# The expert layers as 2 x 2 block products: seven products in place of eight, taken from a growing PSUM bank

## The chip, the cores and the metric

One core of a Trainium2 chip runs the whole program. The metric is the device time of one execution in microseconds (us), lower is better. An execution has five engines that each work through a queue of their own in order: TensorE (PE), VectorE (DVE), ScalarE (ACT), GpSimd (POOL) and the queue that issues transfers (SP). Results of TensorE go to PSUM, which has eight banks here.

## The reference, cut to what matters

An attention block (a linear recurrence with decay, 4 batches, 8 heads, 768 steps, head size 48) gives 3072 rows `x` of 384. Each row is routed to one of eight experts, and the expert is two dense layers in float32:

```
idx  = argmax(cos(x, expert_emb) / tau);  gate = softmax(...)[idx]
for e in range(8):                       # D = 384, F = 1024
    rows = idx == e
    h = maximum(x[rows] @ w1[e], 0)      # (rows x 384) @ (384 x 1024)
    out[rows] = gate[rows] * (h @ w2[e]) # (rows x 1024) @ (1024 x 384)
```

## The kernel before

The attention phase comes first and is not touched, except that two experts ("early", `EARLY = 2`) begin there with rows that are already known. After it `experts` (L1107) goes through eight experts. Each has room for `CAPS[e]` rows: 384, 384, 432, 416, 400, 384, 384, 384. Rows are gathered from DRAM into tiles `G` of 128 rows (`gather`, L994, POOL).

For one expert the work is:

- `turn_x` (L1027): nine or twelve TensorE transposes turn the gathered rows into `xT` (feature on the partitions), for three blocks `m` of 128 features through two PSUM banks `Y`, each copied out by DVE (L1039).
- `layer1` (L1052): for each of eight blocks `f` of 128 hidden units, three matmuls (one per `m`) with 128 x 128 weights of `w1` and all rows of the expert as moving columns, then a Relu on ACT out of PSUM into `hT` (L1049).
- `layer2` (L1074): with 384 rows, for each tile of 128 rows eight matmuls over `f`, each 384 columns wide (L1081), then `finish`: DVE multiplies by the gate (L1062) and POOL scatters the 128 rows to `out` by an indirect transfer (L1063). With more than 384 rows the product is taken turned round (weights `w2` stationary, rows moving, L1089), copied to `yT` by DVE (L1092), and `turn_out` (L1095) transposes four tiles back (L1101) and calls `finish` for each, after the next expert's first layer.

A float32 matmul is two TensorE instructions in the trace, and so are its weight loads (PEld). A transpose is one. The early experts' rows beyond 256 and the transposes for expert 2 come just before `layer2` of experts 0 and 1. From there the order of work on every engine is the program's order, written by hand: layer2(0), layer2(1), then for e = 2 to 7 layer1(e), turn_out(e-1), turn_x(e+1), gathers for e+2, layer2(e), and the loads of the weights of e+2 (`weights`, L975, on SP). The attention phase orders its work by a `Plan`: a list of (planned time, function) that is sorted and emitted. Its planned times only fix the order on each queue.

Of the kernel before, what the change touches and what calls it, by code (L numbers as in the profile page):

```python
# [9 lines left out]
F32 = mybir.dt.float32  # L10
I32 = mybir.dt.int32
ACT = mybir.ActivationFunctionType
ALU = mybir.AluOpType
# [3 lines left out]
B, H, S, D = 4, 8, 768, 48  # L17
DM, E, F = H * D, 8, 1024
N = B * S
# [5 lines left out]
NK = DM // 128  # L25
# [254 lines left out]
def rings(k):  # L280

    nc, pool = k.nc, k.aconst

    def ring(name, count, shape, pad=None, pool=pool):
        out = []
        for i in range(count):
            t = pool.tile(shape, F32, name=f"{name}{i}")
            if pad is not None:
                nc.gpsimd.memset(t[:, :, :, D:DP], 0.0)
            out.append(t)  # L290
        return out
# [12 lines left out]
    k.T = [[pool.tile([128, 2, NP, D], F32, name=f"T{bp}_{i}") for i in range(2)] for bp in range(2)]  # L304

    flat = lambda x: x.rearrange(f"q {' '.join('abcde'[: len(x.shape) - 1])} -> q ({' '.join('abcde'[: len(x.shape) - 1])})")
    k.spare = []
    for x in map(flat, (*k.R, *k.K, *k.Rw, *k.Kw[::-1])):
        k.spare += [x[:, i : i + 384] for i in range(0, x.shape[1] - 383, 384)]
    k.early_x = [  # L310
        flat(of(k.RT, t))[:, 0 : NK * 384].rearrange("q (m i) -> q m i", m=NK) for t in (TURNS - 3, TURNS - 2)
    ]
    k.T1 = [pool.tile([128, 2, NP, D], F32, name=f"Tmid{bp}") for bp in range(2)]
    k.peek = pool.tile([128, 2], F32, name="peek")
    k.sq = ring("sq", 1, [128, DM])
    k.ssq = [k.const.tile([128, B], F32, name=f"ssq{i}") for i in range(2)]
# [648 lines left out]
    plan.emit()  # L965


def weight_tiles(k):
    return (
        k.wp.tile([128, NK, F], F32, name="w1", tag="w1"),  # L970
        k.wp.tile([128, NF, DM], F32, name="w2", tag="w2"),
    )


def weights(k, j, which, pieces=None, paced=False):  # L975
# [28 lines left out]


def x_of(k, e, m):
    return (k.early_x[e] if e < EARLY else k.xT[e % 2])[:, m, :]


def h_of(k, e, f):  # L1010
    return k.spare[e * NF + f] if e < EARLY else k.hT[e % 2][:, f, :]


def turn_tile(k, e, t):

# [11 lines left out]
def turn_x(k, e):  # L1027
    if e < EARLY:
        for t in range(AHEAD, TILES[e]):
            turn_tile(k, e, t)  # L1030
        return
    for m in range(NK):
        ps = k.Y[m % 2]
        for t in range(TILES[e]):
            G, r = k.G[(e % 2) * TM + t], rows_in(e, t)
            k.nc.tensor.transpose(  # L1036
                ps[:, t * 128 : t * 128 + r], G[0:r, m * 128 : (m + 1) * 128], k.ident[0:r, 0:r]
            )
        k.nc.vector.tensor_copy(x_of(k, e, m)[:, 0 : CAPS[e]], ps[:, 0 : CAPS[e]])  # L1039


def first_layer(k, e, f, cols):
    w1 = k.weights[e][0]
    ps = (k.D[3], k.Y[1], k.D[0], k.D[1])[f % 4][:, 0 : cols.stop - cols.start]
    for m in range(NK):
        k.last = k.nc.tensor.matmul(  # L1046
            ps, w1[:, m, f * 128 : (f + 1) * 128], x_of(k, e, m)[:, cols], start=(m == 0), stop=(m == NK - 1)
        )
    k.nc.scalar.activation(h_of(k, e, f)[:, cols], ps, ACT.Relu)  # L1049


def layer1(k, e):  # L1052
    cols = slice(AHEAD * 128 if e < EARLY else 0, CAPS[e])
    for f in range(NF):
        first_layer(k, e, f, cols)


def finish(k, e, t, ps):

    n = rows_in(e, t)  # L1060
    y = k.gp.tile([128, DM], F32, name="y", tag="y")
    k.nc.vector.tensor_scalar_mul(y[0:n], ps[0:n], k.lists[0:n, e, 1, t : t + 1])  # L1062
    k.nc.gpsimd.indirect_dma_start(  # L1063
        out=k.out[:, :], out_offset=IndirectOffsetOnAxis(ap=k.goes[0:n, e, t : t + 1], axis=0),
        in_=y[0:n, :], in_offset=None, bounds_check=N - 1, oob_is_err=False,
    )


def next_bank(k):
    k.turn = 1 - k.turn  # L1070
    return k.U[k.turn]


def layer2(k, e):  # L1074

    n, w2 = CAPS[e], k.weights[e][1]
    if n % 128 == 0:
        for t in range(TILES[e]):
            ps = next_bank(k)[:, 0:DM]
            for f in range(NF):  # L1080
                k.nc.tensor.matmul(  # L1081
                    ps, h_of(k, e, f)[:, t * 128 : (t + 1) * 128], w2[:, f, :], start=(f == 0), stop=(f == NF - 1)
                )
            finish(k, e, t, ps)
        return
    for m in range(NK):
        ps = next_bank(k)[:, 0:n]
        for f in range(NF):
            k.nc.tensor.matmul(  # L1089
                ps, w2[:, f, m * 128 : (m + 1) * 128], h_of(k, e, f)[:, 0:n], start=(f == 0), stop=(f == NF - 1)  # L1090
            )
        k.nc.vector.tensor_copy(k.yT[:, m, 0:n], ps)  # L1092


def turn_out(k, e):  # L1095
    if CAPS[e] % 128 == 0:
        return
    for t in range(TILES[e]):
        ps, n = next_bank(k)[:, 0:DM], rows_in(e, t)
        for m in range(NK):  # L1100
            k.nc.tensor.transpose(  # L1101
                ps[0:n, m * 128 : (m + 1) * 128], k.yT[:, m, t * 128 : t * 128 + n], k.ident
            )
        finish(k, e, t, ps)


def experts(k):  # L1107
    nc = k.nc
    k.turn = 1
    k.xT = [k.gp1.tile([128, NK, max(CAPS)], F32, name=f"xTe{i}") for i in range(2)]  # L1110
    k.hT = [k.gp1.tile([128, NF, max(CAPS)], F32, name=f"hT{i}") for i in range(2)]
    k.yT = k.gp1.tile([128, NK, max(CAPS)], F32, name="yT")
    for e in range(EARLY):
        turn_x(k, e)
    for e in range(EARLY):
        for t in range(TILES[EARLY + e]):
            gather(k, EARLY + e, t)
    nc.gpsimd.drain()
    for e in range(EARLY):
        layer1(k, e)  # L1120
    turn_x(k, EARLY)
    for e in range(E):
        if e >= EARLY:
            layer1(k, e)
            turn_out(k, e - 1)
            if e + 1 < E:
                turn_x(k, e + 1)
            if e + 2 < E:
                for t in range(TILES[e + 2]):
                    gather(k, e + 2, t)  # L1130
            nc.gpsimd.drain()
        if e == E - 1:
            k.tc.mark_branch_hint_location("rest", "LikelyTaken")
        layer2(k, e)
        if e + 2 < E:
            k.weights.append(weight_tiles(k))
            for i in range(2):
                weights(k, e + 2, i)
        if e == EARLY:
            k.left = nc.values_load(k.flag[0:1, 0:1], min_val=0, max_val=1)  # L1140


def needs(k, first):
# [244 lines left out]
def kernel(  # L1388
# [20 lines left out]
    def pool(name, bufs, **kw):  # L1409
        return ctx.enter_context(tc.tile_pool(name=name, bufs=bufs, **kw))  # L1410
# [6 lines left out]
    n.turned = ((n.D[0], n.D[1]), (n.D[2], n.D[3]))  # L1417
    n.rows = n.U
    n.const = pool("const", 1)
    n.wp = pool("wp", 2)  # L1420
# [5 lines left out]
    n.weights = [weight_tiles(n) for _ in range(2)]  # L1426
    n.expert = {}
    n.G = [n.const.tile([128, DM], F32, name=f"G{i}") for i in range(2 * TM)]

# [41 lines left out]
```

## Time and profile before

Three runs took 426.38, 427.07 and 429.15 us, median 427.07. The profiled execution took 427.70 us; its span, from the first instruction to the last, is 425.9 us, so 1.8 us lie around it.

| | busy us | share of span |
|---|---|---|
| PE (matmuls) | 399.3 | 94% |
| DVE | 147.4 | 35% |
| POOL | 124.7 | 29% |
| ACT | 103.1 | 24% |

Busy time of PE in stretches of the span, with DVE and ACT beside it:

| stretch (us) | work | PE busy | DVE | ACT |
|---|---|---|---|---|
| 178 to 211 | transposes for expert 2, layer2(0), layer2(1) | 32.97 of 33.0 | 4.91 | 0.28 |
| 230.4 to 247.9 | layer2(2), 432 rows | 17.50 of 17.5 | 1.81 | 0.00 |
| 264.66 to 268.76 | turn_out(2), turn_x(4) | 3.62 of 4.1 | 3.33 | 0.52 |
| 356.5 to 372 | layer1(6) | 15.50 of 15.5 | 0.62 | 3.43 |
| 404.4 to 420 | layer2(7) | 15.60 of 15.6 | 1.24 | 0.49 |
| 420 to 425.9 | last gate product, last scatter | 0.09 of 5.9 | 0.62 | 0.00 |

A duration of a matmul in the rows is longer than the distance to the next one, because matmuls overlap: 384 columns show 486 ns, and begin every 322 ns. Where TensorE is full, distances are what counts. The granted TensorE clock is 1.00 in all these stretches.

### The profile page before, as it was taken

To read this page: it belongs to the slowest core of one execution; us is meant where nothing else is said; L and a number is where in the kernel's file an instruction comes from. 1 tells how busy PE (TensorE), PEld (TensorE's weight loads), DVE (VectorE), ACT (ScalarE), POOL (GpSimd) and SP (SyncE) were. 2 spreads that over 40 slices of the span, in tenths; PEclk is the share of its full clock that TensorE was granted. 3 is DMA by queue.
4 is the path that set the end of the run, shared out by engine and by line. 5 is a ranking of instruction groups with operands and counts; after the bars stand their busy time and mean duration, and the time that the engine had idled before them with its cause. 6 is when DMAs were issued, how large, how long until landed. Compare 5 with 4: busy or idle time off the path is not lost. (4 is left out here: it accounts for less than half of the span.)

```text
span 425.9 us, 10753 instructions
## 1 busy us (share of the span) xinstructions
PE 399.3 (94%) x4512; PEld 276.7 (65%) x4512; DVE 147.4 (35%) x428; ACT 103.1 (24%) x263; POOL 124.7 (29%) x167
## 2 busy tenths in 40 slices
PE   7879889799998899999999999999999999999994
PEld 3767778798987788855555555555555565555552
DVE  7957577588887540111101100310310211011000
ACT  1345545545555223300021012002101100200200
POOL 2756556275622232211240000240032013201001
PEclk9999999899999899999999999999999999999999
DMA  9999777576125577605564040424416235200001
GB/s 168 189 185 219 163 166 153 118 155 146 42 77 170 145 240 245 209 18 170 203 215 148 0 148 8 179 83 143 164 44 202 69 136 159 99 20 35 0 22 41
DMA packets 94683, 54.28 MB, mean 127 GB/s; under 512 B 77955, under 2 KB 89266, under 8 KB 94626
## 3 DMA queue, kind: packets, MB, share of 16 engines
q1 hardware_dynamic: 88658, 43.67, 37.6%
q0 software_dynamic: 3264, 9.44, 6.6%
q8 instruction: 37, 0.61, 0.6%
q10 hardware_dynamic: 2704, 0.40, 0.6%
q14 instruction: 20, 0.16, 0.1%
HBM read 44.20 MB, written 9.58 MB: 126 GB/s over the span
## 5 line engine op out<-in xcount | busy, mean ns | idle before, releaser
L1063 POOL DMA_INDIRECT out_dram<-y,goes x27 | 26.5, 981 | 204.4 <-DVE y L1062 153.3
L1046 PE MATMUL ps<-xTe,w 128*128 128x384 f32 (+3 forms) x216 | 75.5, 499 | 0.0
L1049 ACT ACTIVATE hT<-ps 128x384 f32<-128x384 f32 (+3 forms) x36 | 18.1, 504 | 184.6 <-PE ps L1046 184.6
L1062 DVE TENSOR_SCALAR y<-pu,lists_sorted 128x384 f32<-128x384 f32 (+3 forms) x27 | 16.1, 614 | 131.9 <-PE pu L1081 83.9
L1046 PEld LDWEIGHTS ps<-xTe,w 128*128 128x128 f32 x216 | 41.0, 190 | 31.5 <-issue 11.9
L1089 PE MATMUL pu<-hT,w 128*128 128x432 f32 (+2 forms) x144 | 51.0, 514 | 0.0
L1081 PE MATMUL pu<-w,hT 128*128 128x384 f32 x144 | 46.9, 486 | 0.0
L1089 PEld LDWEIGHTS pu<-hT,w 128*128 128x128 f32 x144 | 27.1, 190 | 22.0 <-issue 15.3
L1081 PEld LDWEIGHTS pu<-w,hT 128*128 128x128 f32 x144 | 27.2, 190 | 18.5
L999 POOL DMA_INDIRECT G<-xs,take x23 | 23.2, 1008 | 26.2 <-PE py L1019 10.1
L348 POOL TENSOR_TENSOR Rw<-R,rpow 128x384 f32<-128x384 f32 x22 | 22.8, 1036 | 22.7 <-PE ps L390 20.9
L1046 PE MATMUL ps<-RT,w 128*128 128x256 f32 (+1 forms) x144 | 27.1, 340 | 0.4 <-DVE RT L1022 0.4
L1046 PE MATMUL py<-xTe,w 128*128 128x384 f32 (+3 forms) x72 | 26.1, 499 | 0.0
L1039 DVE COPY xTe<-py 128x384 f32<-128x384 f32 (+3 forms) x18 | 10.0, 568 | 44.9 <-PE py L1036 44.4
L390 PE MATMUL ps<-RT,KT 48*64 48x128 f32 x768 | 24.3, 273 | 0.5 <-DVE RT L377 0.5
L1046 PEld LDWEIGHTS ps<-RT,w 128*128 128x128 f32 x144 | 22.6, 197 | 2.5 <-ACT Rw L1049 0.6
L343 POOL TENSOR_TENSOR Kw<-K,kpow 128x384 f32<-128x384 f32 x22 | 23.5, 1066 | 0.0
L390 PEld LDWEIGHTS ps<-RT,KT 48*64 48x64 f32 x768 | 20.9, 133 | 3.1 <-issue 2.1
L1092 DVE COPY yT<-pu 128x432 f32<-128x432 f32 (+2 forms) x9 | 5.3, 591 | 45.4 <-PE pu L1089 45.4
L1046 PEld LDWEIGHTS py<-xTe,w 128*128 128x128 f32 x72 | 13.7, 190 | 10.5 <-issue 4.0
L364 PE MATMUL ps<-ident,Rw 128*128 128x128 f32 x96 | 15.6, 286 | 4.8 <-POOL T L453 2.2
L377 DVE TENSOR_TENSOR RT<-ps,uw 128x512 f32<-128x512 f32 x24 | 16.5, 688 | 9.8 <-ACT RT L371 9.7
(239 smaller groups left out, 532.5 us busy)
## 6 DMA issues: line engine op xcount, KB each, us to landing
w<-in_moe_w_dram SPq DMA_DIRECT2D x24, 512.0 KB, 4.7
w<-in_moe_w_dram SPq DMA_DIRECT2D x32, 384.0 KB, 4.9
K<-in_k_dram SPq DMA_DIRECT2D x24, 192.0 KB, 3.5
V<-in_v_dram SPq DMA_DIRECT2D x24, 192.0 KB, 3.7
xs<-X SPq DMA_DIRECT2D x24, 192.0 KB, 2.5
R<-in_r_dram SPq DMA_DIRECT2D x22, 192.0 KB, 4.4
out_dram<-y,goes POOLq DMA_INDIRECT x27, 2.6
R<-in_r_dram ACTq DMA_DIRECT2D x2, 192.0 KB, 5.2
```

The lines of the kernel that those rows point to most:

```text
L343: q.tensor_mul(of(k.Kw, t)[:, u, :, 0:D], of(k.K, t)[:, u], k.kpow)
L348: ins = q.tensor_mul(of(k.Rw, t)[:, u, :, 0:D], of(k.R, t)[:, u], k.rpow)
L364: k.nc.tensor.transpose(bank[:, p * C : (p + 1) * C], pair(src[:, u], p), k.ident)
L377: k.nc.vector.tensor_mul(of(k.RT, t)[:, u, :, :, 1, :], k.turned[u][0].rearrange("q (p s i) -> q p s i", p=NP, s=2), k.uw[:, :, None, None ...
L390: ins = k.nc.tensor.matmul(k.D[2 * u + par][halves(s), p * C : (p + 1) * C], KT[rows, u, p, halves(s)], RT[rows, u, p, s].rearrange("q j i ...
L999: k.nc.gpsimd.indirect_dma_start(out=G[0:n, :], out_offset=None, in_=k.xs[0:rows, :], in_offset=IndirectOffsetOnAxis(ap=(k.take_first if f ...
L1046: k.last = k.nc.tensor.matmul(ps, w1[:, m, f * 128 : (f + 1) * 128], x_of(k, e, m)[:, cols], start=(m == 0), stop=(m == NK - 1))
L1049: k.nc.scalar.activation(h_of(k, e, f)[:, cols], ps, ACT.Relu)
L1062: k.nc.vector.tensor_scalar_mul(y[0:n], ps[0:n], k.lists[0:n, e, 1, t : t + 1])
L1063: k.nc.gpsimd.indirect_dma_start(out=k.out[:, :], out_offset=IndirectOffsetOnAxis(ap=k.goes[0:n, e, t : t + 1], axis=0), in_=y[0:n, :], in ...
L1081: k.nc.tensor.matmul(ps, h_of(k, e, f)[:, t * 128 : (t + 1) * 128], w2[:, f, :], start=(f == 0), stop=(f == NF - 1))
L1089: k.nc.tensor.matmul(ps, w2[:, f, m * 128 : (m + 1) * 128], h_of(k, e, f)[:, 0:n], start=(f == 0), stop=(f == NF - 1))
```

## The change

Each layer is cut into 2 x 2 blocks and multiplied with seven block products in place of eight (Strassen's scheme in Winograd's form). Sums and differences of blocks of both operands are made by DVE: `S1`, `T1` for layer 1, `S2`, `T2` for layer 2. In layer 1 only two of the three feature blocks `m` can be paired; the third adds four plain products to a group of four `f` (`group`), so that a group has eleven products of two matmuls at half the rows (192 to 216 columns). In layer 2 two tiles of 128 rows are paired, and halves of 192 output columns: seven products of four matmuls. The third tile, or the 144 to 176 rows beyond 256, stays plain (`third`, `columns`).

The partial sums that several outputs share are not multiplied again. A PSUM bank "a" grows through the products, and ACT copies it at three states to `kept` (`keep`); two more banks "b" and "c" take the rest, and DVE adds `kept` to them on the way out (`add`), three additions in a group. Relu of those three outputs then runs on ACT from SBUF in place. The banks come from a ring of six (`ring_bank`).

The copies of the transposed rows go from DVE to ACT (`copy_x`), and `turn_m` places the third block of transposes after the first matmuls of layer 2. `turn_out` handles two tiles in place of four. All of this stands in one `Plan` with planned times. Weight buffers are fixed pairs, `h` of odd experts and `S2` lie in attention's `RT` buffers.

```diff
-    k.spare = []
-    for x in map(flat, (*k.R, *k.K, *k.Rw, *k.Kw[::-1])):
-        k.spare += [x[:, i : i + 384] for i in range(0, x.shape[1] - 383, 384)]
+    k.spare_two = [
+        flat(x)[:, 0:768].rearrange("q (f i) -> q f i", f=2) for x in (*k.R, *k.K, *k.Rw, *k.Kw[::-1])
+    ]
...
-def weight_tiles(k):
-    return (
-        k.wp.tile([128, NK, F], F32, name="w1", tag="w1"),
-        k.wp.tile([128, NF, DM], F32, name="w2", tag="w2"),
-    )
+def weight_tiles(k, i):
+    return k.wp.tile([128, NK, F], F32, name=f"w1_{i}"), k.wp.tile([128, NF, DM], F32, name=f"w2_{i}")
...
-    return k.spare[e * NF + f] if e < EARLY else k.hT[e % 2][:, f, :]
+    return h_one(k, e, f)
...
-def layer1(k, e):
-    cols = slice(AHEAD * 128 if e < EARLY else 0, CAPS[e])
+def layer1_rest(k, e):
     for f in range(NF):
-        first_layer(k, e, f, cols)
-def finish(k, e, t, ps):
+        first_layer(k, e, f, slice(AHEAD * 128, CAPS[e]))
+def ring_bank(k):
+    k.turn = (k.turn + 1) % 6
+    return (*k.D, *k.U)[k.turn]
+def plus(k, out, a, b, op=ALU.add):
+    k.nc.vector.tensor_tensor(out, a, b, op)
+def left_sums(k, s, a, i):
+    (a11, a12), (a21, a22) = a
+    plus(k, s[i], *((a21, a22), (s[0], a11), (a11, a21), (a12, s[1]))[i], ALU.subtract if i else ALU.add)
+def right_sums(k, t, b, i):
+    (b11, b12), (b21, b22) = b
+    plus(k, t[i], *((b12, b11), (b22, t[0]), (b22, b12), (b21, t[1]))[i], ALU.subtract)
+def w1_block(k, e, i, m):
+    return k.weights[e][0][:, m].rearrange("q (g i c) -> q i g c", g=2, i=2)[:, i]
+def sum_w1(k, e, i):
+    s = [k.S1[:, j] for j in range(4)]
+    left_sums(k, s, [[w1_block(k, e, r, m) for m in range(2)] for r in range(2)], i)
+def half_of(k, e, m, c):
+    h = CAPS[e] // 2
+    return x_of(k, e, m)[:, c * h : (c + 1) * h]
+def sum_x(k, e, i):
+    h = CAPS[e] // 2
+    if i == 4:
+        plus(k, k.T1[:, 4, 0:h], half_of(k, e, 2, 0), half_of(k, e, 2, 1), ALU.subtract)
+        return
+    t = [k.T1[:, j, 0:h] for j in range(4)]
+    right_sums(k, t, [[half_of(k, e, m, c) for c in range(2)] for m in range(2)], i)
+def copy_x(k, e, m):
+    k.nc.scalar.copy(x_of(k, e, m)[:, 0 : CAPS[e]], k.xbank[m][:, 0 : CAPS[e]])
+def turn_m(k, e, m):
+    ps = k.xbank[m] = k.Y[m % 2]
+    for t in range(TILES[e]):
+        G, r = k.G[(e % 2) * TM + t], rows_in(e, t)
+        k.nc.tensor.transpose(
+            ps[:, t * 128 : t * 128 + r], G[0:r, m * 128 : (m + 1) * 128], k.ident[0:r, 0:r]
+        )
+def group(k, plan, e, g, at):
+    nc, h = k.nc, CAPS[e] // 2
+    x = CAPS[e] / 384
+    p = Net()
+    def put_at(t, fn, *args):
+        plan.at(at + t * x, fn, *args)
+    def view(ps):
+        return ps[:, 0 : 2 * h].rearrange("q (i c) -> q i c", i=2)
+    def times(name, a, b, start=False):
+        if start:
+            setattr(p, name, ring_bank(k))
+        ps = getattr(p, name)
+        for i in range(2):
+            k.last = nc.tensor.matmul(
+                ps[:, i * h : (i + 1) * h], a[:, g, i * 128 : (i + 1) * 128], b,
+                start=start and i == 0, stop=True, skip_group_check=True,
+            )
+    def A(i, m):
+        return w1_block(k, e, i, m)
+    def S(i):
+        return k.S1[:, i - 1]
+    def T(i):
+        return k.T1[:, i - 1, 0:h]
+    def Bm(m, c):
+        return half_of(k, e, m, c)
+    def keep(i):
+        nc.scalar.copy(k.kept[i][:, 0 : 2 * h], p.a[:, 0 : 2 * h])
+    def out(i, c):
+        return h_group(k, e, g)[:, 2 * i : 2 * i + 2, c * h : (c + 1) * h]
+    def add(name, i, c, j):
+        plus(k, out(i, c), view(getattr(p, name)), view(k.kept[j]))
+    def relu(i, c):
+        nc.scalar.activation(out(i, c), out(i, c), ACT.Relu)
+    put_at(0.0, times, "a", A(0, 0), Bm(0, 0), True)
+    put_at(0.66, times, "b", A(0, 1), Bm(1, 0), True)
+    put_at(1.3, times, "b", A(0, 2), Bm(2, 0))
+    put_at(0.8, keep, 0)
+    put_at(1.95, times, "a", S(2), T(2))
+    put_at(2.6, times, "c", A(1, 2), Bm(2, 1), True)
+    put_at(2.05, add, "b", 0, 0, 0)
+    put_at(2.7, keep, 1)
+    put_at(3.25, times, "a", S(1), T(1))
+    put_at(3.3, relu, 0, 0)
+    put_at(3.9, times, "c", S(3), T(3))
+    put_at(4.0, keep, 2)
+    put_at(4.55, times, "a", S(4), Bm(1, 1))
+    put_at(4.65, add, "c", 1, 1, 2)
+    put_at(5.2, times, "a", A(0, 2), Bm(2, 1))
+    put_at(5.3, relu, 1, 1)
+    put_at(5.85, times, "c", A(1, 1), T(4))
+    put_at(6.0, lambda: nc.scalar.activation(out(0, 1), view(p.a), ACT.Relu))
+    put_at(6.5, times, "c", A(1, 2), T(5))
+    put_at(7.2, add, "c", 1, 0, 1)
+    put_at(7.8, relu, 1, 0)
+GROUP = 7.17
+def h_group(k, e, g):
+    return k.h[e % 2][g][:, :, 0 : CAPS[e]]
+def h_two(k, e, f):
+    if e < EARLY:
+        x, i = k.spare_two[(e * NF + f) // 2], 2
+        return x
+    return h_group(k, e, f // 4)[:, f % 4 : f % 4 + 2]
+def h_one(k, e, f):
+    return h_two(k, e, f - f % 2)[:, f % 2]
+def sum_h(k, e, i):
+    for q in (0, 2):
+        a = [[h_two(k, e, 4 * j + q)[:, :, t * 128 : (t + 1) * 128] for j in range(2)] for t in range(2)]
+        if e < EARLY or q == 0:
+            n = 2 if e < EARLY else 4
+            if n == 4:
+                a = [[h_group(k, e, j)[:, :, t * 128 : (t + 1) * 128] for j in range(2)] for t in range(2)]
+            left_sums(k, [k.S2[:, j, q : q + n] for j in range(4)], a, i)
+def w2_block(k, e, j, c):
+    return k.weights[e][1][:, 4 * j : 4 * j + 4, c * 192 : (c + 1) * 192]
+def sum_w2(k, e, i):
+    right_sums(
+        k, [k.T2[:, j] for j in range(4)], [[w2_block(k, e, j, c) for c in range(2)] for j in range(2)], i
+    )
+def gates(k, e, t):
     n = rows_in(e, t)
-    y = k.gp.tile([128, DM], F32, name="y", tag="y")
-    k.nc.vector.tensor_scalar_mul(y[0:n], ps[0:n], k.lists[0:n, e, 1, t : t + 1])
+    return k.lists[0:n, e, 1, t : t + 1]
+def send(k, e, t, y):
+    n = rows_in(e, t)
     k.nc.gpsimd.indirect_dma_start(
         out=k.out[:, :], out_offset=IndirectOffsetOnAxis(ap=k.goes[0:n, e, t : t + 1], axis=0),
         in_=y[0:n, :], in_offset=None, bounds_check=N - 1, oob_is_err=False,
     )
-def next_bank(k):
...
+def finish(k, e, t, ps):
+    n = rows_in(e, t)
+    y = k.gp.tile([128, DM], F32, name="y", tag="y")
+    k.nc.vector.tensor_scalar_mul(y[0:n], ps[0:n], gates(k, e, t))
+    send(k, e, t, y)
+def layer2(k, plan, e, at):
+    nc = k.nc
+    p = Net()
+    p.y, p.columns = {}, {}
+    w2 = k.weights[e][1]
+    rest = CAPS[e] - 256
+    half = 192
+    def put_at(t, fn, *args):
+        plan.at(at + t, fn, *args)
+    def times(name, a, b, start=False):
+        if start:
+            setattr(p, name, ring_bank(k))
+        ps = getattr(p, name)[:, 0:half]
+        for q in range(4):
+            k.last = nc.tensor.matmul(
+                ps, a(q), b[:, q], start=start and q == 0, stop=True, skip_group_check=True,
+            )
+    def A(t, j):
+        return lambda q: h_one(k, e, 4 * j + q)[:, t * 128 : (t + 1) * 128]
+    def S(i):
+        return lambda q: k.S2[:, i - 1, q]
+    def T(i):
+        return k.T2[:, i - 1]
+    def keep(i, t):
+        nc.scalar.mul(k.kept[i][:, 0:half], p.a[:, 0:half], gates(k, e, t))
+    def out(t, c):
+        if t not in p.y:
+            p.y[t] = k.gp.tile([128, DM], F32, name="y", tag="y")
+        return p.y[t][:, c * half : (c + 1) * half]
+    def add(name, t, c, j):
+        nc.vector.scalar_tensor_tensor(
+            out(t, c), getattr(p, name)[:, 0:half], gates(k, e, t), k.kept[j][:, 0:half], ALU.mult, ALU.add
+        )
+    def third(js):
+        if js[0] == 0:
+            p.z = ring_bank(k)[:, 0:DM]
+        for f in js:
+            k.last = nc.tensor.matmul(
+                p.z, h_one(k, e, f)[:, 256:384], w2[:, f, :], start=(f == 0), stop=(f == NF - 1)
+            )
+    def columns(m):
+        p.columns[m] = ring_bank(k)[:, 0:rest]
+        for f in range(NF):
+            k.last = nc.tensor.matmul(
+                p.columns[m], w2[:, f, m * 128 : (m + 1) * 128], h_one(k, e, f)[:, 256 : CAPS[e]],
+                start=(f == 0), stop=(f == NF - 1),
+            )
+    def columns_out(m):
+        nc.vector.tensor_copy(k.yT[:, m, 0:rest], p.columns[m])
+    z = 2.6
+    if rest == 128:
+        put_at(0.0, third, range(0, 4))
+        put_at(9.1, third, range(4, NF))
+        put_at(11.8, lambda: finish(k, e, 2, p.z))
+    else:
+        for m, t in enumerate((0.0, 9.1, 10.2)):
+            put_at(t, columns, m)
+            put_at(t + 2.7, columns_out, m)
+    put_at(z + 0.0, times, "a", A(0, 0), w2_block(k, e, 0, 0), True)
+    put_at(z + 1.3, times, "b", A(0, 1), w2_block(k, e, 1, 0), True)
+    put_at(z + 1.4, keep, 0, 0)
+    put_at(z + 2.6, times, "a", S(2), T(2))
+    put_at(z + 2.7, add, "b", 0, 0, 0)
+    put_at(z + 3.9, times, "c", S(3), T(3), True)
+    put_at(z + 4.0, keep, 1, 1)
+    put_at(z + 5.2, times, "a", S(1), T(1))
+    put_at(z + 6.6, keep, 2, 1)
+    put_at(z + 7.0, add, "c", 1, 1, 2)
+    put_at(z + 9.2, times, "a", S(4), w2_block(k, e, 1, 1))
+    put_at(z + 10.5, times, "c", A(1, 1), T(4))
+    put_at(z + 10.6, lambda: nc.scalar.mul(out(0, 1), p.a[:, 0:half], gates(k, e, 0)))
+    put_at(z + 10.7, lambda: send(k, e, 0, p.y[0]))
+    put_at(z + 11.9, add, "c", 1, 0, 1)
+    put_at(z + 12.0, lambda: send(k, e, 1, p.y[1]))
+LAYER2 = 14.5
+def turn_out(k, e, t):
+    ps, n = ring_bank(k)[:, 0:DM], rows_in(e, t)
     for m in range(NK):
-        ps = next_bank(k)[:, 0:n]
...
+        k.nc.tensor.transpose(
+            ps[0:n, m * 128 : (m + 1) * 128], k.yT[:, m, (t - 2) * 128 : (t - 2) * 128 + n], k.ident
+        )
+    finish(k, e, t, ps)
 def experts(k):
     nc = k.nc
-    k.turn = 1
+    k.turn = 5
     k.xT = [k.gp1.tile([128, NK, max(CAPS)], F32, name=f"xTe{i}") for i in range(2)]
-    k.hT = [k.gp1.tile([128, NF, max(CAPS)], F32, name=f"hT{i}") for i in range(2)]
-    k.yT = k.gp1.tile([128, NK, max(CAPS)], F32, name="yT")
+    wide = [k.gp1.tile([128, NF // 2, max(CAPS)], F32, name=f"hT{i}") for i in range(2)]
+    rt = [x.rearrange("q u p s j i -> q (u p s j i)") for x in k.RT]
+    k.h = [wide, [x.rearrange("q (f i) -> q f i", f=4) for x in rt[0:2]]]
+    k.S2 = rt[2].rearrange("q (j f i) -> q j f i", j=4, f=4)
+    k.yT = k.gp1.tile([128, NK, max(CAPS) - 256], F32, name="yT")
+    k.S1 = k.gp1.tile([128, 4, 2, 256], F32, name="S1")
+    k.T1 = k.gp1.tile([128, 5, max(CAPS) // 2], F32, name="Tx")
+    k.T2 = k.gp1.tile([128, 4, 4, 192], F32, name="T2")
+    k.kept = [k.gp1.tile([128, max(CAPS)], F32, name=f"kept{i}") for i in range(3)]
+    k.xbank = {}
     for e in range(EARLY):
-        turn_x(k, e)
+        for t in range(AHEAD, TILES[e]):
+            turn_tile(k, e, t)
     for e in range(EARLY):
         for t in range(TILES[EARLY + e]):
             gather(k, EARLY + e, t)
     nc.gpsimd.drain()
     for e in range(EARLY):
-        layer1(k, e)
-    turn_x(k, EARLY)
+        layer1_rest(k, e)
+    plan = Plan()
+    at = 0.0
     for e in range(E):
         if e >= EARLY:
-            layer1(k, e)
...
+            for g in range(2):
+                group(k, plan, e, g, at + g * GROUP * CAPS[e] / 384)
+            if CAPS[e - 1] > 384:
+                plan.at(at + 4.6, turn_out, k, e - 1, 2)
+                plan.at(at + 5.2, turn_out, k, e - 1, 3)
+            for i, t in enumerate((0.6, 2.8, 5.4, 8.0)):
+                plan.at(at + t, sum_w2, k, e, i)
+            at += 2 * GROUP * CAPS[e] / 384
+        nxt = {0: 2, 1: None}.get(e, e + 1)
+        if nxt is not None and nxt < E:
+            for m in range(NK):
+                plan.at(at + (0.0, 0.4, 2.7)[m], turn_m, k, nxt, m)
+                plan.at(at + (0.45, 0.9, 3.0)[m], copy_x, k, nxt, m)
+            for t in range(TILES[nxt + 1] if EARLY <= e and nxt + 1 < E else 0):
+                plan.at(at + 3.1, gather, k, nxt + 1, t)
+            for i in range(5):
+                plan.at(at + (4.0, 5.8, 6.2, 7.6, 8.4)[i], sum_x, k, nxt, i)
+            at += 0.9
+        plan.at(at + 0.8, nc.gpsimd.drain)
+        if e < EARLY:
+            for i in range(4):
+                plan.at(at + 0.1 + 2.0 * i, sum_w2, k, e, i)
+        for i in range(4):
+            plan.at(at + (0.3 if e + 1 < E else 1.0) + i * 0.65, sum_h, k, e, i)
+        layer2(k, plan, e, at)
+        if e + 1 < E and e >= 1:
+            for i in range(4):
+                plan.at(at + (8.0, 8.7, 9.8, 10.5)[i], sum_w1, k, e + 1, i)
         if e == E - 1:
-            k.tc.mark_branch_hint_location("rest", "LikelyTaken")
-        layer2(k, e)
+            plan.at(at - 0.1, k.tc.mark_branch_hint_location, "rest", "LikelyTaken")
+        at += LAYER2 + (2.4 if CAPS[e] > 384 else 0.7)
         if e + 2 < E:
-            k.weights.append(weight_tiles(k))
             for i in range(2):
-                weights(k, e + 2, i)
+                plan.at(at - 0.05, weights, k, e + 2, i)
         if e == EARLY:
-            k.left = nc.values_load(k.flag[0:1, 0:1], min_val=0, max_val=1)
+            plan.at(at - 0.04, left, k)
+    plan.emit()
...
+    sets = [weight_tiles(n, i) for i in range(2)]
+    n.weights = [sets[e % 2] for e in range(E)]
```

More of the change, by code (lines that the diff above doesn't have):

```diff
@@ L1024, in turn_tile @@
     )
[L1027 to L1039, printed above, removed]
 def first_layer(k, e, f, cols):
@@ L1066, in finish @@
     )
-def next_bank(k):
[L1070 to L1085, printed above, removed]
-    for m in range(NK):
-        ps = next_bank(k)[:, 0:n]
[L1088 to L1092, printed above, removed]
@@ L1095, in turn_out @@
[L1095 to L1104, printed above, removed]
+def finish(k, e, t, ps):
[3 more added lines that the diff above has]
+    send(k, e, t, y)
@@ L1119, in experts @@
     for e in range(EARLY):
-        layer1(k, e)
-    turn_x(k, EARLY)
+        layer1_rest(k, e)
+    plan = Plan()
+    at = 0.0
     for e in range(E):
         if e >= EARLY:
-            layer1(k, e)
[L1125 to L1131, printed above, removed]
+            for g in range(2):
[26 more added lines that the diff above has]
+                plan.at(at + (8.0, 8.7, 9.8, 10.5)[i], sum_w1, k, e + 1, i)
@@ L1143, in needs, with left @@
+    plan.emit()
+def left(k):
+    k.left = k.nc.values_load(k.flag[0:1, 0:1], min_val=0, max_val=1)
 def needs(k, first):
@@ L1419 @@
     n.const = pool("const", 1)
-    n.wp = pool("wp", 2)
+    n.wp = pool("wp", 1)
     n.xs = tc.dram_tile([N, DM], F32, name="xs")
@@ L1425 @@
     n.need_dram = tc.dram_tile([E, TG], I32, name="need_dram")
-    n.weights = [weight_tiles(n) for _ in range(2)]
+    sets = [weight_tiles(n, i) for i in range(2)]
+    n.weights = [sets[e % 2] for e in range(E)]
     n.expert = {}
```

## The prediction

> **What bounds the kernel now.** I read the page's engine shares first, then the busy time by stretches, then the timeline of TensorE (PE) where stages meet, then the waits and the timeline of POOL. The first two say where the time is.
>
> ```profile
> PE 399.3 (94%) x4512; PEld 276.7 (65%) x4512; DVE 147.4 (35%) x428; ACT 103.1 (24%) x263; POOL 124.7 (29%) x167
> ```
>
> ```profile
> 356.50:372.00 15.50, 15.50 (x50) 9.09 (x49) 0.62 (x1) 3.43 (x7) 3.83 (x4) 1.00 0.48 164
> ...
> 404.40:420.00 15.60, 15.60 (x49) 8.93 (x47) 1.24 (x2) 0.49 (x1) 1.96 (x2) 1.00 0.07 28
> ```
>
> Columns of the second: stretch, its length, busy time of PE, PEld, DVE, ACT, POOL (instructions in brackets), granted clock, DMA share, GB/s. First and second layers are PE from end to end, at clock 1.00, while DVE and ACT are nearly idle. So from 178 us on the time is a number of PE instructions times their distance. That distance is in the timeline, where a group's first instruction follows the last of the group before:
>
> ```profile
> 158.08 4.05 PE L1046 MATMUL ps<-RT,w 128*128 128x256 f32 x18
> 161.97 1.46 PE L1046 MATMUL py<-RT,w 128*128 128x256 f32 x6
> ...
> 168.39 2.09 PEld L1046 LDWEIGHTS ps<-RT,w 128*128 128x128 f32 x18
> ...
> 168.50 2.17 PE L1046 MATMUL ps<-RT,w 128*128 128x128 f32 x18
> ...
> 170.51 0.83 PE L1046 MATMUL py<-RT,w 128*128 128x128 f32 x6
> ```
>
> 256 columns: (161.97 - 158.08)/18 = 0.2161 us. 128 columns: (170.51 - 168.50)/18 = 0.1117 us, although each has new weights whose load shows 192 ns: loads overlap too. 384 columns: layer1(6) takes 15.48 us for 48, 0.3225. The line through the first two gives 0.1639 at 192, 0.170, 0.177, 0.1835 at 200, 208, 216 and 0.125, 0.138, 0.151 at 144, 160, 176. No 192-wide matmul is in the trace: half of 0.3225 = 0.161 bounds it below, and above it the weight-load row of 0.190, if loads ceased to overlap. I take 0.1639, between two measured neighbours.
>
> **First layers.** A group had 12 float32 products of 384 columns (24 instructions, 7.74 us) and now has 11 x 2 of 192 (44 instructions): 44 x 0.1639 = 7.21. An expert of 384 rows: 88 x 0.1639 = 14.42 for 15.48, saves 1.06, three times. 432, 416, 400 rows: 16.15, 15.57, 14.99 for 17.40, 16.76, 16.12, saves 1.25, 1.19, 1.13. Sum 6.75.
>
> **Second layers.** 384 rows: the third tile 16 x 0.3225 = 5.16, products 7 x 4 x 2 x 0.1639 = 9.18, together 14.34 for 15.48; 1.14 saved, five times. Larger experts: 48 x 0.151 + 9.18 = 16.42 for 17.51, then 15.79 for 16.86, 15.17 for 16.12. Sum 8.8.
>
> **Transposes.** Here the trace has real gaps of PE:
>
> ```profile
> 265.86 1.04 PE L1101 MATMUL pu<-ident,yT 128*128 128x128 f32 x6 [0.39 <-DVE y L1062]
> ...
> 305.18 0.55 PE L1036 MATMUL py<-ident,G 128*128 128x128 f32 x3 [0.55 <-DVE xTe L1039]
> ```
>
> `turn_x` has two banks for three blocks and waits for DVE's copy. From first transpose to next stage it takes 2.05, 2.00, 2.02, 1.76, 1.76, 1.52 = 11.1 us. With the third block moved behind layer 2's first matmuls (2.6 us, against copies of 0.49) the wait is gone: 12 or 9 transposes of 0.112, 3 x 1.3 + 3 x 1.0 = 6.9. Saves 4.2. `turn_out` takes 2.08, 2.07, 2.06 = 6.2; six transposes from a ring of six banks take 0.67, in all 2.0. Saves 4.2. So PE has 24.0 us less to do.
>
> **What is added on DVE and ACT.** DVE additions: 384 elements with one PSUM operand took 0.553 us, 512 took 0.688 us; so 768 take about 0.96. An expert has 4 x 0.96 (w2) + 8 x 0.69 (w1, h) + 5 x 0.36 (x) + 6 x 0.55 + 4 x 0.36 (outputs), some 16 us of 30: hidden under PE, whose queue needs the sums late: `S2` is due 5.2 us into layer 2, and its two h sums, which wait for the last Relu, end near 3. ACT has per group three copies and four Relus of 0.49 = 3.4 of 7.2 us. Where that cover is thin is expert 1: its w2 sums can't start before layer2(0) has released `T2`, and the order puts 0.96 x 2 and three pairs of 0.43 ahead of `T(3)`: ready near 7.0, due at 6.5. I charge 0.5 us. `sum_w1` needs w1 eight microseconds earlier than before, but SP issued those loads a stage or more ahead. A DVE copy less per transposed block and an ACT copy more change nothing on PE.
>
> **The copies of bank "a".** This is a new wait on the path. Between the products that ACT must copy (`keep(1)`, `keep(2)`) PE has only one other product, 4 x 0.1639 = 0.656 us. The chain to cover:
>
> ```profile
> 392.83 5.97 PE L1046 MATMUL ps<-xTe,w 128*128 128x384 f32 x18
> 393.09 0.49 ACT L1049 ACTIVATE hT<-py 128x384 f32<-128x384 f32 x1 [1.45 <-PE py L1046]
> ```
>
> ACT starts 0.26 after the product's last instruction gave way, takes 0.49, and PE goes on some 0.07 after a release (265.19 + 0.60 of DVE, then 265.86). 0.82 - 0.656 = 0.17 us lost, 2 x 12 groups: 4.1 us. Bounds: 0.1 each where ACT starts 0.20 later (as after 256 columns), 2.4; a whole product's time each where nothing overlaps, 15.7. Behind a waiting matmul all of PE waits; behind a `keep` the next Relu does. `keep(0)` has two products between, and layer 2 at least 1.3 us against the shorter 192-column copy: no wait. Ends of Relus don't block `keep(2)`: `add` of bank "b" ends about 2.7, the Relu at 3.9, `keep(2)` is due at 4.3 in the group.
>
> **The tail.** Here the change pays back:
>
> ```profile
> 276.26 0.98 POOL L1063 DMA_INDIRECT out_dram<-y,goes  x1 [2.34 <-DMA out_dram<-y,goes]
> 279.60 0.91 POOL L1063 DMA_INDIRECT out_dram<-y,goes  x1 [2.36 <-DMA out_dram<-y,goes]
> ...
> 415.86 0.98 POOL L1063 DMA_INDIRECT out_dram<-y,goes  x1 [4.18 <-DVE y L1062]
> 421.02 0.98 POOL L1063 DMA_INDIRECT out_dram<-y,goes  x1 [4.17 <-DVE y L1062]
> ```
>
> A scatter waits until the one before has landed: 3.34 us from one to the next when they come together. Now the last expert's come a tile (5.16 us) apart, and the last starts 1.1 after PE ends (419.92). After the change all three are sent late: the third tile ends 11.7 us into layer 2, its scatter starts 1.1 later at 12.8, `send` of tile 0 at 16.15, of tile 1 at 19.5, while PE ends at 14.3. That is 5.2 after PE in place of 1.1: costs 4.1 us. In the other experts the same queue holds up only gathers wanted a whole expert later.
>
> **The sum.** 24.0 - 4.1 - 0.5 - 4.1 = 15.3 us. From the profiled execution's 427.7 (span 425.9 and 1.8 around it): 412.4. The median of the runs is 0.6 lower, so 412.
>
> The Trainium skill, page "TensorE: Matmul & The Clock Gate", section "Back-to-back issue gap", speaks against narrow matmuls: in a real stream of weight loads and matmuls it gives about 81 ns per 128-column pass, where the isolated gap is 56. By the row above a 128-column instruction takes 0.1117 us, two passes of 56, so this trace agrees with the isolated gap; by the stream figure an estimate of 25 ns more on each of 976 narrow instructions would add 24 us and make the change slower, near 436.
>
> **Rivals.**
> - Slower: weight loads pace the narrow matmuls. Place: all 6 x 88 + 8 x 56 = 976 of them; price 0.190 - 0.1639 each, 25.5 us, giving 438. It decides from a distance of 0.1639 + 15.3/976 = 0.180. For it: PEld's 190 ns exceeds 164. Against it: 128-wide ones run at 0.1117 with such loads.
> - No gain to speak of: each of the 24 copies costs a whole product, because ACT or DVE is held up in its queue (a Relu that waits for an `add` behind a 0.96 us sum stands ahead of the next `keep`). Sum 24.0 - 15.7 - 0.5 - 4.1, giving 424. For it: ACT and DVE run in order and depend on each other there. Against it: about 1 us of slack in the order above.
> - Faster still: copies cost nothing and the last scatters don't queue, 427.7 - 24 = 404. Against it: both delays are measured rows.
> - That the products aren't saved can't be: per pair seven replace eight in the code.
>
> **How the numbers follow.** The forecast has 0.58, its own range 408 to 417. The faster rival 0.12, no gain 0.17, weight pace 0.08, and 0.05 for something slower unseen. The range 404 to 423 leaves out the pace rival and part of the third. A measurement of this kernel tells about 1% (4.3 us) from no change: faster by more takes forecast, faster rival and the no-gain cases that keep 5 us, 0.82; within 1% 0.07; slower 0.11.
>
> **What would show it.** Right: PE instructions 4512 + 240 + 288 - 18 = 5022; 192-wide matmuls 0.164 apart; layer 1 of expert 6 about 14.8 us, layer 2 14.3; two PE waits of 0.1 to 0.2 for ACT in a group; three scatters at the end 3.3 apart and about 5 us between PE's end and the last one's start. Wrong: a distance near 0.19, waits of PE for DVE's sums, copies that wait behind a Relu, or the clock below 1.00 after 178 us.

## The result, and the profile after

The changed kernel takes 416.57 us in the median (415.08 to 418.19, four runs) against 427.69 (426.38 to 429.15) of the kernel before in the same comparison. The ratio is 0.974, with a 95% interval of 0.9683 to 0.9797. The forecast was 412, in a range of 404 to 423. The profiled execution took 415.42 us, its span is 413.6, against 427.70 and 425.9: 12.3 us less (11.1 between the medians), where the sum gave 15.3. One run of the experiments below (layer 1 plain, 421.6 us) was in a slow state and is left out of that kernel's median and ratio.

The page's engine line first:

```profile
PE 385.6 (93%) x5022; PEld 344.3 (83%) x5022; DVE 228.6 (55%) x580; ACT 141.0 (34%) x349; POOL 127.3 (31%) x167
```

PE has the 5022 instructions that were counted beforehand: 510 more than before, and shorter ones. The added work is on DVE (147.4 to 228.6 us busy) and ACT (103.1 to 141.0). The stretches of layer1(6), layer1(7), layer2(7) and of what follows PE's end, with the same columns as before (stretch, length, then busy time of PE, PEld, DVE, ACT and POOL, granted clock, DMA):

```profile
342.51:357.76 15.25, 15.25 (x90) 14.17 (x90) 6.67 (x10) 6.16 (x13) 1.97 (x2) 1.00 0.23 79
373.00:388.25 15.25, 15.25 (x90) 14.19 (x89) 6.67 (x10) 6.16 (x13) 1.97 (x2) 1.00 0.10 39
388.25:402.51 14.26, 14.26 (x74) 12.01 (x72) 4.60 (x8) 2.20 (x5) 0.98 (x1) 1.00 0.01 2
402.51:413.60 11.09, 0.17 (x2) 0.00 (x0) 0.42 (x1) 0.00 (x0) 1.96 (x2) 0.62 0.16 58
```

The second layer fell from 15.48 to 14.26 us, the first only from 15.48 to 15.25, and PE's end is now followed by 11.09 us, where it was 5.98 (425.90 - 419.92).

Where PE waits can hardly be seen as PE's own idle time. It shows in the starts. This is layer1(7) in the timeline:

```profile
382.57 0.81 PE L1115 MATMUL ps<-Tx,S 128*128 128x192 f32 x4
...
383.22 0.81 PE L1115 MATMUL ps<-xTe,w 128*128 128x192 f32 x4
383.48 0.48 ACT L1133 COPY kept<-ps 128x384 f32<-128x384 f32 x1 [1.17 <-PE ps L1115]
...
384.01 1.27 PEld L1115 LDWEIGHTS ps<-Tx,S 128*128 128x128 f32 x8 [0.27 <-ACT kept L1133]
384.01 1.57 PE L1115 MATMUL ps<-Tx,S 128*128 128x192 f32 x8
385.02 0.48 ACT L1133 COPY kept<-ps 128x384 f32<-128x384 f32 x1 [0.64 <-PE ps L1115]
385.55 0.62 PEld L1115 LDWEIGHTS ps<-xTe,S 128*128 128x128 f32 x4 [0.27 <-ACT kept L1133]
```

The product from 382.57 takes 0.65 us to the next start. ACT starts its copy 0.26 after that, is done at 383.96, and the product into bank "a" begins at 384.01, when 383.87 would have been its turn: a wait of 0.14. Then ACT's second copy starts at 385.02, again 0.26 after the product gave way, so that product took until 384.76: 0.75 us for 0.65. The first weight load after the wait starts together with the matmul and not ahead of it, and the next start is another 0.1 late. Together 0.24 us for each of the two copies of a group. In the three larger experts, whose products are longer, it is 0.19 to 0.23, and in the first groups of experts 3 and 4 the transposes of `turn_out` stand between the second copy and the next product into bank "a", which is then not late: 22 of the 24 copies cost time, 4.9 us in all.

The end of the program, PE and POOL:

```profile
399.91 1.46 PE L1245 MATMUL pu<-w,RT 128*128 128x192 f32 x8
...
401.01 0.98 POOL L1214 DMA_INDIRECT out_dram<-y,goes  x1 [21.84 <-DVE y L1224]
...
401.21 1.46 PE L1245 MATMUL ps<-T,RT 128*128 128x192 f32 x8
...
404.58 0.98 POOL L1214 DMA_INDIRECT out_dram<-y,goes  x1 [2.59 <-ACTq L1614]
408.69 0.98 POOL L1214 DMA_INDIRECT out_dram<-y,goes  x1 [3.12 <-DMA out_dram<-y,goes]
```

The last product starts at 401.21 and gives way 1.30 later, at 402.51. The last scatter starts 6.18 us after that, in place of 1.1, because it stands behind two others, each of which waits for the one before to land.

### The profile page after: what moved, and what is told of

The parts are those of the page before. It is cut to its first block, busy times and chain, and to the rows that moved or that the text cites. A ratio compares the mean times of both kernels' runs of the same rounds, so it can differ in the third digit from the quotient of the medians.

```text
span 413.6 us, 12129 instructions
## 1 busy us (share of the span) xinstructions
PE 385.6 (93%) x5022; PEld 344.3 (83%) x5022; DVE 228.6 (55%) x580; ACT 141.0 (34%) x349; POOL 127.3 (31%) x167
## 5 line engine op out<-in xcount | busy, mean ns | idle before, releaser
L996 POOL DMA_INDIRECT G<-xs,take x23 | 23.7, 1031 | 35.4 <-issue 10.3
L1115 PE MATMUL ps<-xTe,w 128*128 128x192 f32 (+3 forms) x160 | 31.4, 333 | 0.0
L1115 PEld LDWEIGHTS ps<-xTe,w 128*128 128x128 f32 x160 | 27.5, 190 | 0.0
L1245 PE MATMUL ps<-T,RT 128*128 128x192 f32 x144 | 25.4, 326 | 0.0
L1245 PEld LDWEIGHTS ps<-T,RT 128*128 128x128 f32 x144 | 23.7, 190 | 0.0
L371 ACT COPY RT<-ps 128x512 f32<-128x512 f32 x24 | 14.1, 589 | 20.2 <-PE ps L364 19.2
L1115 PE MATMUL ps<-Tx,S 128*128 128x192 f32 (+3 forms) x96 | 20.3, 341 | 0.0
L1133 ACT COPY kept<-ps 128x384 f32<-128x384 f32 (+3 forms) x24 | 11.7, 489 | 22.7 <-PE ps L1115 19.7
L405 DVE TENSOR_TENSOR AT<-ps,smask 128x256 f32<-128x256 f32 x48 | 18.5, 412 | 1.4 <-PE ps L390 1.4
L412 DVE COPY_PREDICATED AT<-dmask,ps 128x256 f32<-128x256 int32 x48 | 18.5, 438 | 0.0
L364 PE MATMUL ps<-ident,Kw 128*128 128x128 f32 x96 | 14.9, 276 | 3.3 <-POOL Kw L343 1.5
```

The lines of the kernel that those rows point to most:

```text
L364: k.nc.tensor.transpose(bank[:, p * C : (p + 1) * C], pair(src[:, u], p), k.ident)
L405: k.nc.vector.tensor_mul(of(k.AT, t)[:, u, par].rearrange("q (p i) -> q p i", p=NP), kinds(k, u, par)[:, :, 0], k.smask[:, None, :].to_bro ...
L412: k.nc.vector.copy_predicated(of(k.AT, t)[:, u, par].rearrange("q (p i) -> q p i", p=NP), k.dmask[:, None, :].to_broadcast([128, NP, HC]), ...
L996: k.nc.gpsimd.indirect_dma_start(out=G[0:n, :], out_offset=None, in_=k.xs[0:rows, :], in_offset=IndirectOffsetOnAxis(ap=(k.take_first if f ...
L1115: k.last = nc.tensor.matmul(ps[:, i * h : (i + 1) * h], a[:, g, i * 128 : (i + 1) * 128], b, start=start and i == 0, stop=True, skip_group ...
L1245: k.last = nc.tensor.matmul(ps, a(q), b[:, q], start=start and q == 0, stop=True, skip_group_check=True,)
```

## The experiments

The attention phase ends at other times from execution to execution: the transposes for expert 2 start between 176.9 and 183.8 us in the profiles here (177.9 before, 178.5 after). The last three rows of the table were measured on another chip than the four above them: the kernel before took 433.39 us in the median there and 429.39 here, and the three starts are 181.5 to 183.8, the others 176.9 to 179.8. From there on PE's stages repeat to about 0.02 us. So the kernels are compared below by two lengths from their profiles: the expert stretch, from the first transpose for expert 2 to the point at which PE's last product gives way, and the tail, from there to the start of the last scatter. The ratios of times are to the kernel before in the same comparison, with 95% intervals.

| kernel | expert stretch | tail | sum | median of runs | ratio |
|---|---|---|---|---|---|
| before | 242.04 | 1.10 | 243.1 | | |
| changed | 223.98 | 6.18 | 230.2 | 416.57 | 0.974 (0.9683 to 0.9797) |
| last layer 2 plain | 225.22 | 1.09 | 226.3 | 413.11 | 0.9637 (0.9575 to 0.9699) |
| groups interleaved | 218.58 | 6.63 | 225.2 | 409.72 | 0.9554 (0.9483 to 0.9624) |
| copies elsewhere | 219.04 | 6.08 | 225.1 | 410.89 | 0.9571 (0.9501 to 0.9642) |
| layer 1 plain | 225.97 | 6.78 | 232.8 | 416.95 | 0.9751 (0.9641 to 0.9860) |
| arrangement only | 235.73 | 1.88 | 237.6 | 427.26 | 0.9869 (0.9807 to 0.9930) |
| full transposes | 221.78 | 5.86 | 227.6 | 416.08 | 0.9602 (0.9550 to 0.9654) |
| three edits together | 217.59 | 1.10 | 218.7 | 407.80 | 0.9402 (0.9361 to 0.9443) |

The theory at the start: the matmuls save what was counted, two thirds of layer 1's saving goes to PE's waits for ACT's copies of bank "a", and some 5 us go to the queue of scatters at the end. The rival for the first: narrow matmuls or the sums on DVE eat the gain. For the second: the end of the program is late by itself.

**The scatters at the end.** The last expert's second layer goes back to plain tiles:

```diff
-        layer2(k, plan, e, at)
+        if e == E - 1:
+            plain2(k, plan, e, at)   # for t in 0, 1, 2: eight matmuls of 384 columns, then finish(k, e, t, ps)
+        else:
+            layer2(k, plan, e, at)
```

In this kernel the first tiles of the last expert stand in the order ahead of its last Relu, so part of the hidden values that they read is not that of the reference; the instructions are the same.

> Only the last expert's second layer goes back to three plain tiles of 8 matmuls, each scattered when it is done. Theory (scatters to the output wait for one another, and the block scheme sends all three at the end): PE ends 15.48 - 14.26 = 1.2 us later, but the last scatter starts 1.1 us after PE's end in place of 6.2, so the span falls by 3.9 us, from 413.6 to about 409.7. Rival (the late last scatter comes from the end of the program itself, not from the order of the three): it stays 5 to 6 us after PE's end and the span grows by about 1 us, to 414.8.

Its timeline at the end:

```profile
399.89 5.32 PE L1321 MATMUL ps<-w,RT 128*128 128x384 f32 x16
...
400.98 0.98 POOL L1214 DMA_INDIRECT out_dram<-y,goes  x1 [4.17 <-DVE y L1224]
...
406.14 0.98 POOL L1214 DMA_INDIRECT out_dram<-y,goes  x1 [4.18 <-DVE y L1224]
```

PE gives way at 399.89 + 5.16 = 405.05, the last scatter follows after 1.09, and it waits for DVE and no longer for another scatter. From the start of layer2(7) to the last scatter it is 16.57 us, against 20.44: 3.87 us, as expected. The order of the first tiles is not what gains: in the last kernel below the tiles stand behind the last Relu, and the same stretch takes 16.58 us. (The span is 410.9 because this execution's expert stretch began 1.3 us later.) The rival falls.

**The copies, by order.** The two groups of a first layer alternate, with three more `kept` buffers:

```diff
-                group(k, plan, e, g, at + g * GROUP * CAPS[e] / 384)
+                group(k, plan, e, g, at + g * 0.65 * CAPS[e] / 384)
...
-        plan.at(at + t * x, fn, *args)
+        plan.at(at + (2 * t + o) * x, fn, *args)   # t: start of the product, o: distance of copy, add or Relu behind it
...
-    ps, n = ring_bank(k)[:, 0:DM], rows_in(e, t)
+    ps, n = k.Y[t % 2][:, 0:DM], rows_in(e, t)
```

> The two groups of a first layer are interleaved product by product, with a set of kept buffers each, so that at least two and mostly three products lie between a product that ACT must copy and the next one into the same bank; turn_out uses the two transpose banks. The same products, additions, copies. Theory (each copy costs PE about 0.24 us, a wait of 0.13 and a restart of 0.11): layer 1 of expert 6 goes from 15.25 to about 14.35 us, all six from 94.7 to about 89.5, the span from 413.6 to about 408.3. Rival (the first layers' gain is eaten by the sums on DVE or by the narrow matmuls themselves): layer 1 of expert 6 stays near 15.2 and the span within 1 us of 413.6, or grows if ACT and DVE now fall behind.

```profile
341.28 1.46 PE L1117 MATMUL ps<-Tx,S 128*128 128x192 f32 x8
342.58 1.46 PE L1117 MATMUL pu<-xTe,w 128*128 128x192 f32 x8
343.88 1.46 PE L1117 MATMUL ps<-Tx,S 128*128 128x192 f32 x8
345.18 1.46 PE L1117 MATMUL pu<-Tx,S 128*128 128x192 f32 x8
```

Each line holds eight instructions and gives way to the next after 1.30 us: no start is late. Layer1(6) takes 14.30 us, all six first layers 89.35 in place of 94.74, the expert stretch falls by 5.40. The same matmuls, sums and copies take 0.95 us less in layer1(6), where no `turn_out` stands, only by their order and their `kept` buffers, so it was the wait.

**The copies, by taking the wait away.** The copies of states two and three read from SBUF:

```diff
-        nc.scalar.copy(k.kept[i][:, 0 : 2 * h], p.a[:, 0 : 2 * h])
+        if i:
+            nc.scalar.copy(view(k.kept[i]), k.T1[:, 0:2, 0:h])
+        else:
+            nc.scalar.copy(k.kept[i][:, 0 : 2 * h], p.a[:, 0 : 2 * h])
```

> The second and third copy in each group read the sums in T1 in place of bank a, so ACT has the same work but PE has nothing to wait for (the output of the first layers is then not the reference's). Theory: the waits and restarts of PE go, layer 1 of expert 6 from 15.25 to about 14.3 us, the span from 413.6 to about 408.3. Rival (narrow matmuls or DVE's sums are what costs): no change in layer 1, span 413 to 414.

```profile
343.80 1.46 PE L1115 MATMUL ps<-Tx,S 128*128 128x192 f32 x8
345.10 0.81 PE L1115 MATMUL ps<-xTe,S 128*128 128x192 f32 x4
345.75 0.81 PE L1115 MATMUL ps<-xTe,w 128*128 128x192 f32 x4
```

Eight instructions to the next start now take 1.30 us, where the same pair took 1.54 (384.01 to 385.55) in the changed kernel. Layer1(6) is 14.30 us here too, with ACT about as busy as in the changed kernel (6.07 us against 6.16). Two different edits give one number, 88 instructions at 0.1625 us.

**Layer 1 plain.** The groups go back to three full-width matmuls for each block `f`, with Relu straight from PSUM and no sums for layer 1:

```diff
-    put_at(0.0, times, "a", A(0, 0), Bm(0, 0), True)
...
+    for j in range(4):                                  # three matmuls of all rows, then a Relu from the bank
+        plan.at(at + 1.935 * j * x, block, j)
+        plan.at(at + (1.935 * j + 2.1) * x, relu, j)
```

> Only the first layers go back to plain products (24 float32 matmuls of full width per expert, Relu straight from PSUM, no sums for layer 1); all else as in the changed kernel. Theory (the block products of layer 1 save 6.4 us of matmuls and give 5 back): the first layers take 96.7 us in place of 94.7 and the span is about 415.6. Rival (they give what the count of columns says): span about 420.

```profile
343.20:358.68 15.48, 15.48 (x50) 9.07 (x49) 3.98 (x5) 3.43 (x7) 1.98 (x2) 1.00 0.23 80
```

The expert stretch grows by 1.99 us. As the change stands, block products in six first layers are worth 2 us, and 7.4 us once their waits are gone (96.73 here against 89.35 interleaved). The runs' times can't show the 2 us: the ratios 0.9751 and 0.974 lie within each other's intervals.

**The arrangement without block products.** Both layers plain, the rest as in the changed kernel:

```diff
-    put_at(z + 0.0, times, "a", A(0, 0), w2_block(k, e, 0, 0), True)
...
+    for t in range(2):                                  # eight matmuls of 384 columns, then finish
+        put_at(z + 0.1 + 3.2 * t, tile, t)
```

> Both layers go back to plain products (layer 2: two plain tiles in place of the seven products, the third tile or the columns beyond 256 as in the changed kernel); what stays is the rearrangement: ACT's copies of the transposed rows, the third block moved behind layer 2's first matmuls, two tiles in turn_out, the ring of six banks. Theory (the rearrangement alone gives 2.7 + 4.2 us of PE, and spaced scatters keep the old tail of 1.1 us): span about 425.9 - 6.9 = 419 us. Rival (the gaps of the transposes only move into other waits): span 424 to 426.

The expert stretch is 6.3 us shorter than before, close to the 6.9 expected. The rest of the changed kernel's 18.1 us, 11.75, comes from the block products: 2.0 in layer 1 and some 9.7 in layer 2 (9.2 against the second layers of before, which have fewer late starts behind transposes). The span of this execution is 425.2 because its attention phase ended 3.9 us later than before's; the ratio of the times, 0.987, carries the gain: 5.5 us in stretch and tail are 1.3% of 433. Its tail is 0.8 us longer than before's, as two scatters come together there.

**Short transposes.** The last tile of a larger expert has 16 to 48 rows:

```diff
-            ps[:, t * 128 : t * 128 + r], G[0:r, m * 128 : (m + 1) * 128], k.ident[0:r, 0:r]
+            ps[:, t * 128 : (t + 1) * 128], G[:, m * 128 : (m + 1) * 128], k.ident
```

> The changed kernel, but the last tile's transposes of the larger experts take all 128 rows of the tile in place of the 16 to 48 that are used. Theory (the transposes saved 2.7 and not 4.2 us because each short one costs an extra 0.17 us before its weight load): the first eight plus the last four transposes for an expert of 432 rows go from 1.25 + 0.59 to 0.90 + 0.45 us, three such experts, 1.5 us in all; span about 412.1. Rival (the larger time is the restart of PE between stages): no change in these stretches.

The changed kernel:

```profile
225.99 1.32 PE L1092 MATMUL py<-ident,G 128*128 128x128 f32 x8
...
226.41 0.48 PEld L1092 LDWEIGHTS py<-ident,G 32*128 32x128 f32 x4 [0.17 <-issue]
...
227.06 0.14 PEld L1092 LDWEIGHTS py<-ident,G 32*128 32x128 f32 x1 [0.17 <-issue]
```

With full transposes:

```profile
228.03 0.98 PEld L1092 LDWEIGHTS py<-ident,G 128*128 128x128 f32 x8
228.21 1.04 PE L1092 MATMUL py<-ident,G 128*128 128x128 f32 x8
```

The eight now end after 0.88 us and not 1.25 (228.21 to 229.09), the four after 0.44 and not 0.60, so transposing more rows takes less time. The gap of 0.17 before the short loads is gone, and so are 0.1 us at the start of the products behind each piece. The expert stretch falls by 2.2 us, more than the 1.5 expected. The runs' times can't confirm this: between comparisons the kernel before moved from 427.69 to 433.39, and the ratio fell by 1.4% where stretch and tail explain 0.6%.

**The three together.**

> Interleaved groups, last expert's second layer plain (its tiles put behind the last Relu in the order), full transposes. The three gains are on different stretches and should add: 4.9 + 3.9 + 1.5 from the changed kernel's 413.6 gives a span of about 403.3. If they cover one another, 405 or more.

```profile
396.22 5.32 PE L1321 MATMUL ps<-w,RT 128*128 128x384 f32 x16
...
402.48 0.98 POOL L1214 DMA_INDIRECT out_dram<-y,goes  x1 [4.13 <-DVE y L1224]
```

Stretch and tail sum to 218.7 us, 11.5 below the changed kernel and 24.5 below the one before; 10.3 were expected from the first. The span, 407.3, is 4 us above the 403.3 expected, because its expert stretch started 5.3 us later than the changed kernel's, and that is no part of the edits. The ratio is 0.940 with an interval of 0.9361 to 0.9443: it beats both kernels.

## Why the prediction was right, and where it was off

- **Narrow matmuls**: 0.1639 us expected at 192 columns, 0.1625 measured (14.30/88). The rival in which the 190 ns weight loads pace them falls at once, and with it the estimate from the stream figure of the Trainium skill's page "TensorE: Matmul & The Clock Gate", section "Back-to-back issue gap". That page's isolated gap, by its formula 82.5 ns a pass at 192 columns, agrees with this trace: 88 instructions with a weight load each run 162.5 ns apart, 81 a pass if an instruction is two passes, as the prediction takes it. The prediction's estimate of 24 us was also mis-worked: it counts two passes in an instruction but adds the 25 ns once.
- **Layer 2**: 8.8 us expected, 9.2 measured (128.0 to 118.8). No wait on a copy, as forecast.
- **Layer 1**: the matmuls save 7.4 us, forecast 6.75. The copies were sized at 0.17 x 24 = 4.1 us; 22 of them cost 0.19 to 0.24 each, 4.9 together. The chain in the sum was nearly right (0.82, measured 0.79); the term left out is the restart after a wait, 0.1. The first layers lose 5.4 in all: the other 0.46 are a wait and its restart in layer1(5), where the gate product of `turn_out` (317.08) stands ahead of an `add` on DVE, and PE's next product into bank "c" waits. The interleaved kernel doesn't have it, the one with the copies elsewhere does (219.04 against 218.58):

```profile
317.08 0.62 DVE L1224 TENSOR_SCALAR y<-ps,lists_sorted 128x384 f32<-128x384 f32 x1 [2.56 <-PE ps L1323]
...
317.62 0.55 DVE L1045 TENSOR_TENSOR RT<-ps,kept 128x384 f32<-128x384 f32 x1
...
318.22 1.57 PE L1115 MATMUL ps<-Tx,w 128*128 128x192 f32 x8 [0.20 <-DVE RT L1045]
```

- The prediction's own list of signs named 14.8 us for layer1(6); its sum gives 14.42 + 4 x 0.17 = 15.1. The measured 15.25 stands against 15.1.
- **Transposes**: 4.2 us forecast, 2.6 measured (11.1 to 8.5). Mis-sized term: twelve transposes at 0.112. They took 1.8 to 1.9 us and not 1.3, because the short ones cost 0.17 more each; the gap stood in the trace of before and was taken for a part of the wait. `turn_out`: 4.2 forecast, 6.20 - 1.97 = 4.2 measured.
- **Expert 1's sums**: 0.5 us charged, none lost; layer2(1) takes 14.26. A pair of DVE's 256-element additions, charged at 0.86 us, shows 0.76 and is followed by the next pair after 0.67: an instruction starts before the last one's row ends.
- **The tail**: 4.1 us forecast, 5.1 measured. The mechanism is shown by the experiment on the scatters. What was mis-sized is their distance: 3.34 in the middle of the kernel, here 3.57 and 4.11. The chain that ended last shows the second of them:

```profile
404.58 3.33 DMA out_dram<-y,goes
407.91 0.03 issue
407.94 0.02 POOLq L1214
407.95 0.51 issue
408.46 0.06 POOLq L1614
408.52 0.16 issue
408.69 0.98 POOL out_dram L1214
```

The transfer took 3.33 us, and 0.78 lie between its landing and the next scatter, instructions of the closing branch (L1614) among them. In the four other kernels with this order at the end the same distance is 4.54, 3.91, 4.45 and 3.75 us and the transfer 3.77, 3.14, 3.68 and 2.98: 0.77 is left each time. In the middle of the changed kernel a scatter lands after 2.6 us in the median, which leaves about as much of 3.34; scatters that come a tile apart land after 2.54 (before) and 2.58 (last layer 2 plain) at the end too. So it is the transfer that took longer, and not the branch; why it did is open.

- **Before the experts**: 0.65 us later than before (178.53 for 177.88), in a part that the change does not touch. The profiles spread by 2.9 us there on one chip and by 7 over both, so this is not explained and needs no cause in the change.

Together: -18.06 in the expert stretch (forecast -19.4), +5.1 in the tail (forecast +4.1), +0.65 ahead of it: -12.3. The 3 us that are missing are a balance: transposes, copies with the other wait, tail and start fell short by some 4.5, the narrow matmuls and expert 1's sums gave 1.5 more than forecast. That the total lies this near to the sum is in part luck; the two main losses, at the copies and in the tail, are where the forecast put them.

## What to carry to other kernels

Where an accumulating bank is copied at several states, count what PE can do between the copied product and the next one into the same bank: here one product of 0.65 us did not cover 0.79 us, and interleaving two independent groups did, at no cost but three buffers. Fewer products pay in full only where PE's order stays free of waits (7.4 us against 2.0 in the first layers), so price the restart with the wait. And look at what a new order does to the last outputs of the program: three scatters that wait for one another took back 5 of 18 us, and giving up 1.2 us of saving in the last layer brought 5 back.

## What the runs showed of the hardware

- A float32 matmul instruction of 192 columns with new weights each time runs every 0.1625 us, though its weight load shows 190 ns.
- After a wait of PE for ACT, the weight load starts with the matmul and not ahead of it; the product (four instructions of 192 columns) then takes 0.75 to 0.76 us in place of 0.65. The same 0.1 shows behind short transposes, without a wait.
- Among transposes of 128 rows, which follow each other every 0.11 us, one of 16 to 48 rows costs more than another full one: its weight load comes 0.17 us late.
- DVE additions of 768 float32 elements took 0.95 us, of 512 took 0.69, as the line through the shorter rows of before gave.
- An ACT copy of 192 columns scaled by a per-row gate took 0.42 us, a plain one of 384 took 0.48.
- An indirect scatter of 128 rows that waits for the one before starts 0.73 to 0.78 us after that one has landed; it lands 2.6 us after its start in the middle of the program, and 3.0 to 3.8 us after it for the second of three at the end.
